# Block 0 of an attention and SwiGLU kernel: k and v loaded in 4 positions by 128 partitions, one root for both halves

## The chip, the cores and the metric

The kernel runs on one core of a Trainium2 chip. The metric is the device time in microseconds (us); the kernel before took 1040.91 us, the median of three runs (1040.91 to 1042.02). One profiled execution of it lasted 1040.28 us, with a span of 1038.5 us in the trace.

The engines are called by their short names: PE (TensorE, matrix products; PEld is its weight load), DVE (VectorE), ACT (ScalarE), POOL (GpSimd), SP (SyncE, which here only issues DMAs).

## What is computed

The reference has two parts. Attention without a softmax, for 8 batches, 8 heads, 576 positions and a head dimension of 64, all in float32:

```
kv  = einsum('bhsd,bhse->bhde', k, v)          # 64 x 64 for each batch and head
o   = einsum('bhsd,bhde->bhse', q, kv)
o   = o / sqrt(mean(o*o, -1) + 1e-6) * g_norm
x   = o with the heads side by side             # 4608 tokens x 512
```

and a SwiGLU layer on these 4608 tokens, with 1536 hidden units. Its three weights come in float64:

```
g   = x @ w_gate;  val = x @ w_val
out = (g * sigmoid(g) * val) @ w_out
```

## The kernel before

The 4608 tokens are worked off in nine blocks of 512 (`NB`, `BLK`). A batch has 576 positions, so block n takes its tokens from batches n-1 and n. `Att(n)` holds the attention of one block, `Ffn(n)` its SwiGLU layer. While the layer of block n runs, attention for block n+1 is fitted in between. From block 1 on the products use a scheme with fewer multiplications (`Up`, `Inner`, `Down`), whose combined weights are made in blocks 0 and 1; block 0 uses plain products (`plain_up`), since its weights only arrive then.

**k^T v.** For each batch, `load_kv(g)` loads k and v for four heads (g = 0, 1), as two pairs of heads j. The 576 positions are cut in two parts r, each on 64 of the 128 partitions, 5 and 4 positions to a partition (`KT` = 5; which part has five alternates with e). That makes 16 DMAs for a batch, each onto 64 partitions. `kv(g)` multiplies them: for each pair j, position c and part r, two matmuls (u, the head in the pair) with 64 rows and 64 columns, each on its own quarter of the PE array. The two parts land in two PSUM tiles; ACT copies the first to SBUF (L292) and DVE adds the second (L293, through the helper at L111). One matmul in float32 appears as two instructions in the trace.

**The head of the kernel.** For block 0 the order is written in `first()`: turn q (transposes on PE with an identity, L307), k^T v, then `half(0)`: the product of q and k^T v for two of the four token tiles (L327), squares on ACT (L338), sums on DVE (L339), `root` (eleven small DVE operations, an inverse square root by three Newton steps, L345 to L357) and `scale` (L364 through the helper at L113). Then q's second half is turned, its product made, and `turn_x(0)` transposes the scaled result (L374) into x, which ACT copies with the gain (L375). The second half's root, scaling and turn (`second()`) come after the first up matmuls `plain_up(0, (0,))`, and the next up group's first half stands between the two halves of the first.

**Weights.** Each float64 weight piece (128x512 words) is loaded by `Words` into one of four `ld` buffers, and `round_to` makes float32 of it: two ACT operations (L144 for the lower word, L146 for the upper), then four on DVE (L147, L152, L153, L157). `weights(upto)` does so for the pieces in the order g0, v0, g1, v1, and so on, and keeps four loads ahead.

**Order.** The instructions of an engine are put in order by a list scheduler that follows the order of the program where operands and buffers allow; it knows nothing of the real chip. `tc.issue_after(ins)` puts everything traced in its block that runs on the engine of `ins` behind `ins` on that engine; it orders one engine's instructions and makes no engine wait for another. DMAs from SP and from ACT (`nc.sync`, `nc.scalar`) are two queues.

Of the kernel before, what the change touches and what calls it, by code (L numbers as in the profile page):

```python
# [8 lines left out]
F32 = mybir.dt.float32  # L9
U32 = mybir.dt.uint32  # L10
I32 = mybir.dt.int32
OP = mybir.AluOpType
ACT = mybir.ActivationFunctionType

P = 128
# [3 lines left out]
def kernel(  # L19
# [41 lines left out]
    nc = tc.nc  # L61

    B, H, S, D = q.shape
    NT, DM = out.shape
    FF = moe_w_gate.shape[1]
    T = 4
    BLK = P * T
    HB = BLK // 2
    HD = DM // 2
    NB = NT // BLK  # L70
    NS = DM // P
    NF = FF // P
    NP = NF // 2
    KT = 5
    LD = 2 * (2 * KT - 1) * D
    eps = 1e-6
    assert NT == B * S and NT == NB * BLK and NB == B + 1 and S - BLK == BLK // B
    assert 2 * D == P and H == 2 * NS and (2 * KT - 1) * D == S and NS == 4

    def pool(name, bufs, **kw):  # L80
        return ctx.enter_context(tc.tile_pool(name=name, bufs=bufs, **kw))
# [37 lines left out]
    class Words:  # L119
# [18 lines left out]
        def round_to(self, dst):  # L138
            halves = self.raw.rearrange("p (f w) -> p f w", w=2)
            low, high = halves[:, :, 0], halves[:, :, 1]  # L140
            room = ring()

            unit = room[:, 0]
            nc.scalar.activation(out=unit, in_=low, func=ACT.Copy, scale=2.0**-51, bias=2.0)  # L144
            mag = room[:, 1].bitcast(U32)
            nc.scalar.activation(out=mag.bitcast(F32), in_=high.bitcast(F32), func=ACT.Abs)  # L146
            nc.vector.tensor_scalar(  # L147
                out=mag.bitcast(F32), in0=mag.bitcast(F32), scalar1=self.LOW, scalar2=self.HIGH,
                op0=OP.max, op1=OP.min,
            )  # L150
            sign = room[:, 2].bitcast(U32)
            nc.vector.tensor_scalar(out=sign, in0=high, scalar1=0x80000000, scalar2=None, op0=OP.bitwise_and)  # L152
            nc.vector.scalar_tensor_tensor(  # L153
                out=mag, in0=mag, scalar=3, in1=sign, op0=OP.logical_shift_left, op1=OP.bitwise_xor
            )
            a, b = self.shape[0], BLK // self.shape[0]
            nc.vector.tensor_tensor(  # L157
                out=dst.bitcast(U32),
                in0=mag.rearrange("p (a b) -> p a b", a=a, b=b),
                in1=unit.bitcast(U32).rearrange("p (a b) -> p a b", a=a, b=b),  # L160
                op=OP.add,
            )
# [3 lines left out]
        "v": (wv, moe_w_val.bitcast(U32).rearrange("(s p) f -> p s f", p=P)),  # L166
        "o": (wo, moe_w_out.bitcast(U32).rearrange("(c p) d -> p c d", p=P)),
    }
    words = {}

    def load_w(name, j):
        src = wviews[name][1]
# [5 lines left out]
    def round_w(name, j):  # L178
        if name == "o":
            dst = wo[:, j : j + 1, :]  # L180
        else:
            dst = wviews[name][0][j // 2][:, :, P * (j % 2) : P * (j % 2 + 1)]
        words.pop((name, j)).round_to(dst)

    class Att:

# [18 lines left out]

        def place_kv(self, g, i):

            n = (2 * g + i) * LD
            if self.n == 0:
                return self.room.rearrange("p f t -> p (f t)")[:, n : n + LD]  # L210
            if self.n == 1 and g == 0:
                return self.room[:, n : n + LD]
            return ld_pool.tile([P, LD], F32, name="ld")

        def load_kv(self, g):


            if self.n == B:
                return
            for i, (views, src) in enumerate(((self.k, k), (self.v, v))):  # L220
                tile_ = self.place_kv(g, i)
                for e in range(2):
                    j, s0 = 2 * g + e, 0
                    for r in range(2):
                        m = KT - (r != e)
                        at = 2 * D * (KT - r) * e
                        t = tile_[r * D : (r + 1) * D, at : at + 2 * D * m].rearrange("p (h x) -> p h x", h=2)
                        queue = nc.scalar if self.n == 0 and i else nc.sync
                        queue.dma_start(
                            out=t,  # L230
                            in_=src[self.n, 2 * j : 2 * j + 2, s0 : s0 + m * D].rearrange("h (p t) d -> p h (t d)", t=m),
                        )
                        views[j, r] = t.rearrange("p h (t d) -> p h t d", t=m)
                        s0 += m * D

        def load_quarters(self, i):

# [35 lines left out]
        def kv(self, g):  # L273


            if self.n == B:
                return
            if g == 0:
                self.kv_ps = [m_psum.tile([P, NS, D], F32, name="m") for _ in range(2)]
            for e in range(2):  # L280
                j = 2 * g + e
                for c in range(KT):
                    for r in range(2):
                        m = KT - (r != e)
                        for u in range(2 if c < m else 0):
                            nc.tensor.matmul(  # L286
                                self.kv_ps[r][u * D : (u + 1) * D, j, :], lhsT=self.k[j, r][:, u, c, :],
                                rhs=self.v[j, r][:, u, c, :], start=(c == 0), stop=(c == m - 1),
                            )
            if g == 1:  # L290
                dst = kvs[self.n % 3]
                nc.scalar.copy(out=dst, in_=self.kv_ps[0])  # L292
                self.kv_made = add(nc.vector, dst, self.kv_ps[1], dst)  # L293

        def turn_q(self, i, pools=None):

# [16 lines left out]
        def product(self, i, pools=None):  # L313

            pools = pools or (m_psum, m_psum)
            self.ps[i] = [pool.tile([P, 2, NS, D], F32, name=pool.name[0]) for pool in pools]  # L320
            for t in range(2):
                for j in range(NS):
                    for b, _, p0, p1 in self.parts(2 * i + t):
                        for p in range(p0, p1, D):
                            for u in range(2):
                                rows = slice(u * D, (u + 1) * D)
                                nc.tensor.matmul(  # L327
                                    self.ps[i][u][p : p + D, t, j, :],
                                    lhsT=self.qt[rows, 2 * i + t, j, p : p + D], rhs=kvs[b % 3][rows, j, :],
                                    start=True, stop=True,  # L330
                                )
            if self.z is None or 0 < self.n < TURNED:
                self.z = st_pool.tile([P, 2, 2, 2, NS], F32, name="z")
            if i == 0:
                self.sq = ring().rearrange("p f (t j d) -> p f t j d", t=2, j=NS)
            for u in range(2):
                sq = self.sq[:, 2 * i + u]
                self.squared = nc.scalar.activation(out=sq, in_=self.ps[i][u], func=ACT.Square)  # L338
                nc.vector.tensor_reduce(out=self.z[:, i, u], in_=sq, axis=mybir.AxisListType.X, op=OP.add)  # L339

        def root(self, i, k=1):

# [84 lines left out]

        def first(self):
            self.turn_q(0, (b_psum, c_psum))
            for g in range(2):  # L430
                self.kv(g)
            self.half(0)
            squared = self.squared
            self.turn_q(1, (b_psum, c_psum))
            with tc.issue_after(self.scaled.ins):
                self.product(1, (b_psum, a_psum))
            self.turn_x(0)
            return squared, self.scaled

        def second(self):  # L440
            self.root(1)
            self.scale(1)
            self.turn_x(1)
            return self.scaled

        def turn(self):
            for i in range(2):
# [536 lines left out]
    def weights(upto):  # L984
        nonlocal rounded
        while rounded < min(upto, len(pieces)):
            load_weights(rounded + 4)
            round_w(*pieces[rounded])
            rounded += 1
# [6 lines left out]
    blocks = [Att(n) for n in range(NB)]  # L996
    blocks[0].room = h_pool.tile([P, NF, BLK], F32, name="h")
    blocks[0].load_q(0)
    for g in range(2):
        blocks[0].load_kv(g)  # L1000
    blocks[0].load_q(1)
    load_weights(4)
    squared, scaled = blocks[0].first()
# [1 line left out]
    for n in range(NB):  # L1005
        ffn = Ffn(n, blocks[n])
        nxt = blocks[n + 1] if n + 1 < NB else None
        if n == 0:
# [1 line left out]
            with tc.issue_after(squared.ins), tc.issue_after(scaled.ins):  # L1010
                weights(2)
            ffn.plain_up(0, (0,))
            scaled = blocks[0].second()
            for f in range(NF):
                with tc.issue_after(scaled.ins), tc.issue_after(blocks[0].copied.ins) if f else ExitStack():
                    weights(2 * (f + 2))
                if f == 1:
                    ffn.plain_up(1, (0,))
                    ffn.plain_up(0, (1,))
                ffn.plain_up(f, (1,)) if f == 1 else ffn.plain_up(f) if f else None  # L1020
            weights(len(pieces))
            pairs = wo.rearrange("p (j e) d -> p e j d", e=2)
            t2(pairs[:, 0, :, HD:DM], pairs[:, 1, :, HD:DM], pairs[:, 0, :, 0:HD])
# [22 lines left out]
            ffn.up({4: third, 8: two_thirds} if nxt else {})  # L1046
        if nxt:
            nxt.turn()
        if n + 2 < NB:
            blocks[n + 2].load_kv(0)  # L1050
        if TURNED - 2 <= n < NB - 2:
            ffn.loads = blocks[n + 2].load_q
# [2 lines left out]
                    ffn.loads(i)  # L1055
        ffn.down(nxt)
        if n == 0:

            with tc.issue_after(nxt.halves[0].ins):
                for j in range(NP):  # L1060
                    t2(wv[j][:, 0:2], wv[j][:, 2:4], wg[j][:, 0:2])
# [31 lines left out]
```

## Time and profile before

| part of the span | us | from |
|---|---|---|
| PE busy | 1011.3 of 1038.5 | busy table |
| DVE busy | 701.3 | busy table |
| ACT busy | 231.8 | busy table |
| first k^T v matmul | 8.47 | order of time |
| first product of q and k^T v | 17.75 | order of time |
| first transposes of x | 25.32 | order of time |
| first up matmul | 29.13 | order of time |
| k^T v of block 1 | 115.81 | order of time |
| k^T v of block 2, first half | 181.86 | order of time |
| PE waits for an ACT result in block 1 | 2.55 before 201.53 | order of time |

How to read it: an engine's busy time says how much it does, not whether anything waits for it. PE is busy for 97% of the span, so time is lost where PE stands still, or where it runs at a lower granted clock. The rows in order of time show the first: each names its start, and in brackets the idle time before it with what ended that. In the head (the first 38 us) many short steps follow one another on PE, ACT and DVE; there the date at which a step starts says more than its length. DMA rows tell when a transfer was issued; when it landed is seen from the instruction that waited for it.

### The profile page before, as it was taken

The page shows a single profiled execution, that of the slowest core. Times are in us where ns is not written, and L with a number is a line of the kernel's source. Part 1 is how long each engine was busy: PE and PEld are TensorE (multiplying, and loading weights), DVE is VectorE, ACT ScalarE, POOL GpSimd, SP SyncE. Part 2 cuts the span into 40 slices and gives each one's busy share as a digit, 9 for nine tenths or more (in the row PEclk, how much of TensorE's full clock was granted, in tenths as well). Part 3 has the DMA queues.
Part 4 walks back from the last instruction along what each step waited for, and adds up shares of the span by engine and source line. Part 5 has one row for each costly group of instructions (what it writes and reads, how often), then busy time and mean ns, then how long its engine had stood idle before and what let it go on. Part 6 is the DMA issues. An engine that isn't in the chain of part 4 may idle for free.

```text
span 1038.5 us, 21544 instructions
## 1 busy us (share of the span) xinstructions
PE 1011.3 (97%) x8588; PEld 907.9 (87%) x8588; DVE 701.3 (68%) x1202; ACT 231.8 (22%) x357; POOL 368.5 (35%) x280
## 2 busy tenths in 40 slices
PE   4899999999999999999999999999999999999998
PEld 3644688788899989998999899988999899989997
DVE  2999696789656866675766666684668566856661
ACT  3666111122212111121111111211122111212110
POOL 0000443435024631563147305640455136512670
PEclk9899999999999999999999999999999999999999
DMA  9689604765468556864676377726862666166611
GB/s 213 184 260 266 164 1 127 186 191 147 129 179 242 135 111 191 243 162 80 197 239 192 59 204 226 222 47 173 250 194 51 164 206 187 29 152 211 191 31 41
DMA packets 255044, 168.16 MB, mean 162 GB/s; under 512 B 124640, under 2 KB 230240, under 8 KB 254944
## 3 DMA queue, kind: packets, MB, share of 16 engines
q1 hardware_dynamic: 228384, 162.45, 56.5%
q10 hardware_dynamic: 26496, 4.33, 2.4%
q8 instruction: 68, 1.11, 0.5%
q14 instruction: 32, 0.26, 0.1%
q0 software_dynamic: 64, 0.00, 0.0%
HBM read 138.02 MB, written 22.41 MB: 154 GB/s over the span
## 4 chain that ended last, share of the span: by engine, by line
PE 91%; DVE 4%; DMA 2%; issue 1%; POOL 1%; ACT 0%; SPq 0%; DVEq 0%; POOLq 0%; ACTq 0%
PE b L662 25%; PE b L513 20%; PE c L662 12%; PE c L513 10%; PE a L662 6%; PE a L513 5%; PE b L956 4%; PE c L956 4%; PE m L286 2%; PE m L327 1%; DMA w<-t 1%; DVE xi L112 1%; DVE r L111 1%; DVE r L112 1%; DMA h<-in_k_dram 1%
## 5 line engine op out<-in xcount | busy, mean ns | idle before, releaser
L111 POOL TENSOR_TENSOR r<-r 128x256 f32<-128x256 f32 (+1 forms) x105 | 110.8, 1061 | 308.5 <-DVE r L111 233.3
L111 DVE TENSOR_TENSOR r<-b,r 128x512 f32<-128x512 f32 (+1 forms) x273 | 161.8, 605 | 64.2 <-PE b L662 59.1
L112 POOL TENSOR_TENSOR t<-wo 128x512 f32<-128x512 f32 x81 | 115.2, 1446 | 195.5 <-DMA t<-in_q_dram 107.8
L111 DVE TENSOR_TENSOR r<-c,r 128x512 f32<-128x512 f32 (+1 forms) x179 | 108.3, 617 | 89.1 <-PE c L662 49.5
L662 PE MATMUL b<-x,t 128*128 128x128 f32 x1092 | 151.0, 275 | 0.0
L662 PEld LDWEIGHTS b<-x,t 128*128 128x128 f32 x1092 | 136.5, 192 | 0.6 <-DVE r L111 0.2
L111 DVE TENSOR_TENSOR r<-a,r 128x512 f32<-128x512 f32 (+1 forms) x99 | 62.4, 630 | 109.2 <-PE a L513 65.8
L662 PE MATMUL c<-xi,t 128*128 128x128 f32 x840 | 112.2, 275 | 0.3 <-DVE xi L111 0.3
L113 POOL TENSOR_TENSOR h<-r 128x1024 f32<-128x1024 f32 (+1 forms) x40 | 81.4, 2050 | 87.6 <-DVE r L111 74.5
L662 PEld LDWEIGHTS c<-xi,t 128*128 128x128 f32 x840 | 102.8, 192 | 0.4 <-DVE xi L111 0.4
L513 PE MATMUL b<-wo,h 128*128 128x256 f32 x432 | 99.4, 382 | 0.1
L513 PE MATMUL b<-t,h 128*128 128x256 f32 x432 | 96.9, 381 | 0.0
L513 PEld LDWEIGHTS b<-t,h 128*128 128x128 f32 x432 | 81.4, 190 | 11.3 <-issue 0.2
L513 PEld LDWEIGHTS b<-wo,h 128*128 128x128 f32 x432 | 80.0, 190 | 12.6 <-DVE h L113 2.5
L676 ACT COPY r<-b 128x512 f32<-128x512 f32 x63 | 36.9, 585 | 212.8 <-PE b L662 212.8
L662 PE MATMUL b<-xi,t 128*128 128x128 f32 x588 | 79.7, 276 | 0.0
L662 PEld LDWEIGHTS b<-xi,t 128*128 128x128 f32 x588 | 72.4, 192 | 0.0
L662 PE MATMUL b<-x,wg 128*128 128x128 f32 x336 | 52.7, 279 | 0.2 <-DVE x L112 0.2
L662 PE MATMUL b<-x,wv 128*128 128x128 f32 x336 | 51.4, 275 | 0.0
L956 PE MATMUL b<-x,wg 128*128 128x512 f32 (+1 forms) x112 | 45.5, 550 | 3.0 <-ACT r L146 1.9
L513 PE MATMUL c<-t,s 128*128 128x256 f32 x216 | 48.3, 380 | 0.0
L513 PE MATMUL a<-wo,h 128*128 128x256 f32 x216 | 48.3, 379 | 0.0
(133 smaller groups left out, 1583.6 us busy)
## 6 DMA issues: line engine op xcount, KB each, us to landing
t<-w SPq DMA_DIRECT2D x336, 256.0 KB, 3.5
out_dram<-r SPq DMA_DIRECT2D x17, 512.0 KB, 3.1
ld<-in_moe_w_gate_dram SPq DMA_DIRECT2D x12, 512.0 KB, 4.8
ld<-in_moe_w_val_dram SPq DMA_DIRECT2D x12, 512.0 KB, 4.8
ld<-in_moe_w_out_dram SPq DMA_DIRECT2D x12, 512.0 KB, 5.3
w<-t SPq DMA_DIRECT2D x18, 256.0 KB, 2.4
w<-xi SPq DMA_DIRECT2D x12, 384.0 KB, 3.1
ld<-in_k_dram SPq DMA_DIRECT2D x26, 160.0 KB, 3.5
```

The source lines that it names most:

```text
L111: add = lambda e, o, a, b: e.tensor_tensor(out=o, in0=a, in1=b, op=OP.add)
L112: sub = lambda e, o, a, b: e.tensor_tensor(out=o, in0=a, in1=b, op=OP.subtract)
L113: mul = lambda e, o, a, b: e.tensor_tensor(out=o, in0=a, in1=b, op=OP.mult)
L286: nc.tensor.matmul(self.kv_ps[r][u * D : (u + 1) * D, j, :], lhsT=self.k[j, r][:, u, c, :], rhs=self.v[j, r][:, u, c, :], start=(c == 0), ...
L327: nc.tensor.matmul(self.ps[i][u][p : p + D, t, j, :], lhsT=self.qt[rows, 2 * i + t, j, p : p + D], rhs=kvs[b % 3][rows, j, :], start=True, ...
L513: nc.tensor.matmul(banks[e][:, e], lhsT=lhsT, rhs=rhs, start=first and i == 0 and (e == 0 or banks[0] is not banks[1]), stop=i == self.ste ...
L662: nc.tensor.matmul(ps[:, i, f], lhsT=self.weight(o, p, f), rhs=self.operand(o, p), start=first and (i, f) == (0, 0), stop=True, skip_group ...
L676: nc.scalar.copy(out=dst, in_=ps)
L956: nc.tensor.matmul(t, lhsT=w[f // 2][:, i, P * (f % 2) : P * (f % 2 + 1)], rhs=x[:, i, of], start=(i == 0), stop=(i == NS - 1),)
```

## The change

**k and v of block 0** are loaded by a function of their own, `load_first_kv`. Positions 0 to 511 go to all 128 partitions, four positions to each, in four DMAs on SP's queue (k and v, four heads each). The last 64 positions go to 64 partitions in four DMAs on ACT's queue. `first_kv` multiplies head by head: four matmuls with 128 rows and 64 columns, and one with 64 rows for the last positions, 40 in all, where there were 72. The result needs no addition: ACT copies four heads, DVE the other four.

**Later batches** are loaded with nine positions to a partition (`KT` = 9), a pair of heads on each 64 partitions: 8 DMAs a batch, where there were 16. `kv(g)` runs over the nine positions with four quarters of the array each time; two ACT copies bring out the result, and the addition on DVE goes.

**One root for both halves.** `first()` makes both products before one `root(0, 2)`, then scales both halves. Between the two products the first weight piece is rounded: on DVE it stands behind the first half's sums and ahead of the second half's. The lower word of a piece is now converted after the upper (L144 and L146 trade places). q's second half is turned behind the first product.

**The first up groups** are plain: both halves of f = 0, then f = 1, without the exchange of before.

**Block 2's first k and v loads** come after `down` of block 0 in the program, where they stood ahead of it.

The purpose is to have the first k^T v sooner, to take DVE work out of the head, and to use all quarters of PE in the later k^T v.

```
+        def load_first_kv(self):
+            room = self.room.rearrange("p f (h x) -> p (f h) x", h=2)
+            most = {"k": room[:, 0:H], "v": room[:, H : 2 * H]}
+            ...
+            for g in range(2):
+                heads, rows = slice(NS * g, NS * (g + 1)), slice(D * g, D * (g + 1))
+                for x, src in (("k", k), ("v", v)):
+                    nc.sync.dma_start(
+                        out=most[x][:, heads], in_=src[0, heads, 0:BLK].rearrange("h (p t) d -> p h (t d)", t=T)
+                    )
+                    nc.scalar.dma_start(out=last[x][rows], in_=src[0, heads, BLK:S].rearrange("h p d -> p h d"))
+        def first_kv(self):
+            banks = [m_psum.tile([P, 2, D], F32, name="m") for _ in range(2)]
+            for h in range(H):
+                j, u = divmod(h, 2)
+                ps = banks[j // 2]
+                for c in range(T + 1):
+                    ...
+                    nc.tensor.matmul(
+                        ps[u * D : (u + 1) * D, j % 2], lhsT=k, rhs=v, start=(c == 0), stop=(c == T)
+                    )
+            nc.scalar.copy(out=kvs[0][:, 0:2], in_=banks[0])
+            nc.vector.tensor_copy(out=kvs[0][:, 2:4], in_=banks[1])
...
         def kv(self, g):
-            for e in range(2):
-                j = 2 * g + e
-                for c in range(KT):
-                    for r in range(2):
-                        m = KT - (r != e)
-                        for u in range(2 if c < m else 0):
-                            nc.tensor.matmul(
...
+            for c in range(KT):
+                for r in range(2):
+                    k, v = self.k[2 * g + r], self.v[2 * g + r]
+                    for u in range(2):
+                        nc.tensor.matmul(
...
-                nc.scalar.copy(out=dst, in_=self.kv_ps[0])
-                self.kv_made = add(nc.vector, dst, self.kv_ps[1], dst)
+                for r in range(2):
+                    nc.scalar.copy(out=dst[:, r], in_=self.kv_ps[r])
...
         def first(self):
             self.turn_q(0, (b_psum, c_psum))
-            for g in range(2):
-                self.kv(g)
-            self.half(0)
-            squared = self.squared
-            self.turn_q(1, (b_psum, c_psum))
-            with tc.issue_after(self.scaled.ins):
+            self.first_kv()
+            self.product(0)
+            with tc.issue_after(self.multiplied.ins):
+                self.turn_q(1, (b_psum, c_psum))
+            with tc.issue_after(self.squared.ins), tc.issue_after(self.summed.ins):
+                weights(1)
+            with tc.issue_after(words_made[-1].ins):
                 self.product(1, (b_psum, a_psum))
+            self.root(0, 2)
+            for i in range(2):
+                self.scale(i)
             self.turn_x(0)
...
             ffn.plain_up(0, (0,))
-            scaled = blocks[0].second()
+            blocks[0].turn_x(1)
             for f in range(NF):
-                with tc.issue_after(scaled.ins), tc.issue_after(blocks[0].copied.ins) if f else ExitStack():
+                with tc.issue_after(blocks[0].copied.ins):
                     weights(2 * (f + 2))
-                if f == 1:
-                    ffn.plain_up(1, (0,))
-                    ffn.plain_up(0, (1,))
-                ffn.plain_up(f, (1,)) if f == 1 else ffn.plain_up(f) if f else None
+                ffn.plain_up(f) if f else ffn.plain_up(0, (1,))
...
-        if n + 2 < NB:
+        if 0 < n < NB - 2:
             blocks[n + 2].load_kv(0)
...
         ffn.down(nxt)
         if n == 0:
+            blocks[2].load_kv(0)
```

## The prediction

> **What bounds the kernel now.** I read the page first: its busy shares and its 40 slices.
>
> ```profile
> PE   4899999999999999999999999999999999999998
> PEclk9899999999999999999999999999999999999999
> ```
>
> TensorE (PE) is full from the second slice on, so outside the first 26 us a change pays only by what it takes off PE. Then I read the busy time by stretches, to see where the hole at the start lies and what DMA moved meanwhile.
>
> ```profile
> 12.00:14.00 2.00, 2.00 (x14) 1.61 (x12) 0.69 (x1) 0.00 (x0) 0.00 (x0) 1.00 1.11 235
> 18.00:20.00 2.00, 0.96 (x64) 0.82 (x55) 0.41 (x1) 1.04 (x2) 0.00 (x0) 1.00 1.08 347
> 22.00:25.00 3.00, 0.17 (x12) 0.04 (x4) 2.60 (x11) 2.78 (x6) 0.00 (x0) 1.00 0.59 184
> 25.00:29.00 4.00, 1.95 (x8) 1.55 (x8) 4.00 (x10) 2.88 (x5) 0.00 (x0) 0.55 0.15 30
> ```
>
> The columns are stretch, length, busy PE, weight loads, DVE, ACT, POOL, granted clock, DMA share, GB/s. k and v arrive at 235 GB/s, while the weights (18 to 20 us) arrive at 347. From 22 to 29 us PE does 2.1 us of work, DVE works nearly throughout, and the clock falls. Third, TensorE alone in order of time (start, length, line, result, tile size, shape, count; in brackets the idle time before and what ended it).
>
> ```profile
> 11.02 1.11 PE L286 MATMUL m<-h 64*64 64x64 f32 x20 [1.68 <-DMA h<-in_k_dram]
> 12.06 1.11 PE L307 MATMUL b<-ident,ld 128*128 128x128 f32 x4
> 13.96 2.93 PE L286 MATMUL m<-h 64*64 64x64 f32 x114
> 25.32 1.95 PE L374 MATMUL m<-ident,r 128*128 128x128 f32 x8 [3.14 <-DVE r L113]
> 29.13 3.48 PE L956 MATMUL b<-x,wg 128*128 128x256 f32 x8 [1.87 <-ACT r L146]
> 115.81 1.28 PE L286 MATMUL m<-xi 64*64 64x64 f32 x69
> ```
>
> k^T v waits for DMA and ends near 16.9; after it come the product (17.75), the root and the scaling, and x^T is turned only at 25.32. Last, the chain of waits, which names the second hole:
>
> ```profile
> 34.43 0.42 DVE h L113
> 34.85 0.34 DVE r L147
> 35.19 0.34 DVE r L152
> 35.52 0.33 DVE r L147
> 35.86 0.60 DVE r L153
> 36.46 0.34 DVE r L152
> 36.80 0.61 DVE wg L157
> 37.45 1.99 PE b L956 x8
> ```
>
> PE waits for a weight piece whose rounding DVE put behind the second root. After 37.45 it runs on, 24 up groups of 8 matmuls of 512 columns at 3.43 us in sum (82.4 us), until k^T v of block 1 at 115.81. So the head is a chain of latencies, and I cost it by one date: the start of that k^T v. Without waits, at full clock, the up work would have had to start at 115.81 - 82.4 = 33.4.
>
> **What the Trainium skill says.** "SBUF — State Buffer", Door 1: a transfer's bandwidth goes by how many SBUF ports its partitions reach, and partitions 64 to 127 lie on other ports than 0 to 63, so 64 partitions reach half of them. The trace agrees in direction: the k and v loads, 64 partitions each, ran at 235 GB/s against 347 for weights on 128. "TensorE: Matmul & The Clock Gate", LDWEIGHTS: loading time goes by columns, not by contraction; so 128 rows by 64 columns should cost what 64 by 64 does. No run here shows that shape. The same page, The HAM clock gate: an idle window of about 3.4 us halves the clock, a busy one restores it, and windows run free of the kernel. The trace agrees: 0.50 between 26 and 32 us, after the hole at 22. "TensorEngine Tiling (Array Packing)", Key Properties: changing the tiling mode drains TensorE. The trace: in block 1, eight matmuls from 180.04 at 216 ns end issuing at 181.77, k^T v starts at 181.86 and the next full-array matmul at 183.17, 1.31 later against 1.14 in the run of k^T v below: 0.09 in, 0.17 out.
>
> **The change, part by part.**
>
> *Loads of block 0.* 2.10 MB of k and v now go to 128 partitions: at 347 GB/s 6.0 us. The last 64 positions (0.26 MB) and the first q (0.52 MB) go in 256-byte rows; the stretches from 4 to 6 us moved 172 to 206 GB/s, I take 190: 4.1 us. From the first byte at 2.0, with 0.7 for landing: heads 0 to 3 at 9.8, all at 12.8, where before the last k came at 16.09. A gain of 3.3 us in data, if PE can use it.
>
> *k^T v of block 0.* One step of a 64-column tile: block 1's first half takes 1.14 us (115.81 to 116.95) for 20 steps of up to four tiles side by side, 57 ns each. At the half clock I take 114: the four transposes from 12.06 took twice what they take later. Forty matmuls are 80 instructions (each is two in the trace), but five for one head lie on the same column half and follow each other: 80 steps, not 40. And each head goes from 128 rows to 64 and back. A change costs between 0 and 0.15 us (the mean of 0.09 and 0.17 is 0.13); I take 0.06, as only the rows change, and keep both ends. Before 15.1 PE is cold, and a head takes 10 x 0.114 + 0.12 = 1.26: from 9.8, 4.2 heads. The other 3.8 take 0.57 + 0.12 = 0.69 each: end at 17.7. The two copies run side by side, about 0.3 (128x256 took 0.37 and 0.42), with hand-overs 0.4: product from 18.1, against 17.6 before, where copy and add took 0.83. The ends are 17.4 and 19.3.
>
> *One root, and the piece between.* From the ready k^T v: product 1.3, squares 0.6 each, the second sum ends at +3.2. ACT then has two copies and the piece's Abs (0.55 each); DVE rounds it in 1.9 (0.34 + 0.34 + 0.60 + 0.61), to +5.9. What is queued behind that on DVE are the sums of the second half, waited for by the root: 1.2, to +7.1. The root, 11 small operations of 0.21 as from 21.60 to 23.97, to +9.5 (twice the elements took 192 ns against 175). Two scalings 1.3, to +10.8. The turn at half clock 1.97 and the second copy 0.7: x is there at +13.5, or 31.6. The second scaling ends at +12.1, so its eight transposes (1.7 cold) lie beside the copies. Removed are one root (2.3) and the hole before 37.45: piece g0 is done, v0 follows the scaling in 2.1, long before its matmuls, and g1 has all of half 0 and half 1 of the first up group (7 us) to be done in. If ACT takes the piece ahead of the copies, +0.65.
>
> *Result for the head.* 31.6 + 82.4, plus the half clock: before, 29.13 to 32.1 cost 1.5; as PE is nearly unbroken from 28.9 on, I take 0.9. k^T v of block 1 starts at 114.9: a gain of 0.9.
>
> *Blocks 1 to 7.* A position group of five and four left 20 steps a half; nine positions are 18. On PE, which is full: 2 x 57 ns x 14 halves = 1.6 us. Their loads are 8 instead of 16 a block, and DVE loses an add of 0.42 for a second short copy on ACT: nothing, as PE runs beside them without a gap. Block 2's first loads, issued from 110 on, are needed at 181.86: their move costs nothing, hidden by 60 us of other work.
>
> Sum: 1040.9 - 0.9 - 1.6 = 1038.4.
>
> **The rivals.**
>
> *The head gives all back (chance 0.28).* The high price of the shape changes (k^T v at 19.3), ACT taking the piece first (+0.65), and a clock window that costs 1.7: 19.3 + 14.15 + 82.4 + 1.7 = 117.5, 1.7 later than now, which the 1.6 of the later blocks repays: 1041.0. For it: 80 steps in a row where four tiles ran side by side. Against: most of them lie before 15.1, when data were missing anyway.
>
> *A new wait in the first up group (0.20).* Half 1 of f = 0 now follows half 0 in the same PSUM bank; before, f = 1 came between. If its matmuls wait for Silu and the DVE multiply, and that stands behind a rounding of 2.0: +2.0 on the case above, and if the tiles already overlap at the seams, only 0.5 comes from the later blocks: 1040.9 + 1.7 + 2.0 - 0.5 = 1044.1, slower. Against: Silu has the wv matmuls to run in, the multiply the next wg ones.
>
> *Block 1's hole closes too (0.10).* PE stands 2.55 us before 201.53, behind a DVE and DMA chain, and then runs 3.4 us at clock 0.50 (1.7 lost). If the shifted start lets that chain through: 1038.4 - 4.2 = 1034.2. Against: nothing in that chain is touched.
>
> **How the numbers follow.** The forecast has 0.42, the likeliest, and gives the time. Range 1034.4 to 1043.6: it takes in the rival that gives back, both prices of the shape change (-0.7, +1.2) and the clock window's phase (about 1.5 either way), and leaves half of each outer case. Faster: 0.42 + 0.10 = 0.52; same 0.28; slower 0.20.
>
> **What would show it.** The last k of block 0 near 13 us and GB/s near 350 before it; k^T v as 80 instructions with no DMA wait in its second half, ending near 17.7; one set of 11 root operations, ending near 27.6; the first 128x256 up matmul near 31.6 and no wait for a rounding after it; k^T v of block 1 near 114.9; and in later blocks 1.03 us for each half. A k^T v ending past 19, or a wait of PE on ACT or DVE after the first up group, would make it wrong.

## The result, and the profile after

The changed kernel took 1050.99 us (median; 1049.97 to 1053.46) against 1040.97 for the one before: ratio 1.0097, with a 95% interval of 1.0079 to 1.0116. It is 10 us slower, where 1038.4 had been forecast. The page shows where to look. In the first slice (26 us) PE is fuller than before, in the second emptier, and the second has lost clock as well; a dent in the ninth lies at waits that before had too.

```profile
PE   6699999989999999999999999999999999999998
...
PEclk9799999999999999999999999999999999999999
```

PE alone in order of time, with the columns of the same view above:

```profile
10.43 11.51 PE L241 MATMUL m<-h 128*64 128x64 f32 x79 [3.44 <-DMA h<-in_v_dram]
...
22.43 1.97 PE L350 MATMUL m<-kv,r 64*64 64x64 f32 x56 [0.16 <-DVE kv L245]
...
34.21 1.97 PE L397 MATMUL m<-ident,r 128*128 128x128 f32 x8 [6.96 <-DVE r L113]
36.10 2.90 PE L978 MATMUL b<-x,wg 128*128 128x256 f32 x8
...
40.56 1.04 PE L397 MATMUL m<-ident,r 128*128 128x128 f32 x8
...
45.41 4.63 PE L978 MATMUL b<-x,wg 128*128 128x256 f32 x8 [2.34 <-DVE wg L157]
...
126.78 1.28 PE L309 MATMUL m<-xi 64*64 64x64 f32 x72
```

Three things are to be seen. k^T v runs for 11.5 us without a wait, and ends at 22.0, where 17.7 had been forecast. After the products PE stands 6.96 us until the root and the scaling are through (3.14 before, for the first half alone). And after the first half of the first up group there is a second hole, of 2.34 us, for the rounding of a weight piece. k^T v of block 1, the date by which the prediction counted, starts at 126.78 instead of 115.81: 11.0 later. The rest of the span gives 1.3 back, since the spans differ by 9.7 (1048.2 against 1038.5).

The busy time by stretches (columns as above) shows the data side of the first stage:

```profile
10.00:14.00 4.00, 3.57 (x27) 3.13 (x28) 0.00 (x0) 0.00 (x0) 0.00 (x0) 1.00 1.20 298
14.00:18.00 4.00, 4.00 (x29) 3.30 (x29) 0.00 (x0) 0.27 (x1) 0.00 (x0) 1.00 1.13 319
...
27.00:34.00 7.00, 0.25 (x19) 0.11 (x8) 6.23 (x18) 2.71 (x6) 0.00 (x0) 0.80 0.45 145
...
45.00:52.00 7.00, 6.59 (x14) 4.63 (x15) 4.80 (x10) 5.13 (x10) 0.00 (x0) 0.53 0.93 289
```

From 10 to 14 us DMA moves 298 GB/s, where the prediction had read 235 before; taken from 8 to 12, while the last of k and v are under way, it is 323 and 346, against 237 and 231 before. The last of k and v landed at 13.4 instead of 16.1, so the loads do what they were meant to do. (The 319 behind that are q's second half and weights.) But PE, "busy" for the whole of 14 to 18 us, gets only 29 instructions done in it: 138 ns each, where the single 64-column step was priced at 57 (full clock) or 114 (half). From 45 to 52 us the granted clock is 0.53: the second hole was followed by a stretch at half clock, where before had full clock. (The profile has no clock record ahead of the first change of the clock, at 24.3 us here, and prints 1.00; that the clock was half until then is read from lengths. The product from 22.43 takes 1.97 us, and 1.15 in a run where the clock was up.)

What set the second hole is told by the chain of waits of this stretch (start, length, what):

```profile
39.00 1.73 PE c L978 x8
40.72 0.45 PE m L397 x4
41.20 0.48 ACT x L398
...
42.35 0.68 ACT r L145
43.05 0.43 DVE r L147
...
43.82 0.60 DVE r L153
...
44.75 0.61 DVE wg L157
45.37 0.04 issue
45.41 0.79 PE b L978
```

The second half of x is turned only behind the first 16 up matmuls; ACT copies it; only then does ACT get to its share of piece g1 (L145), then DVE rounds it, then PE goes on.

### The profile page after: what moved, and what is told of

Same layout as the page of the kernel before. It is cut to its first block, busy times and chain, and to the rows that moved or that the text cites. A ratio compares the mean times of both kernels' runs of the same rounds, so it can differ in the third digit from the quotient of the medians.

```text
span 1048.2 us, 21289 instructions
## 1 busy us (share of the span) xinstructions
PE 1019.2 (97%) x8508; PEld 910.0 (87%) x8508; DVE 700.2 (67%) x1183; ACT 231.9 (22%) x363; POOL 369.1 (35%) x280
## 4 chain that ended last, share of the span: by engine, by line
PE 92%; DVE 5%; DMA 1%; issue 1%; ACT 0%; SPq 0%; POOL 0%; DVEq 0%; POOLq 0%; ACTq 0%
PE b L684 25%; PE b L535 20%; PE c L684 12%; PE c L535 10%; PE a L684 6%; PE a L535 5%; PE b L978 4%; PE c L978 4%; PE m L309 2%; PE m L350 1%; PE m L241 1%; DVE xi L112 1%; DVE r L112 1%; DMA h<-in_v_dram 1%; PE m L397 1%
```

## The experiments

Two questions: why k^T v takes 11.5 us, and why so much is lost behind it. A change of shape is one from 128 rows to 64 or back, counted here as two for each group of 64-row matmuls; the last group is followed by the product, which has 64 rows too, so 15 of the 16 lie within k^T v. Times are medians; before ran beside each, at 1040.3 to 1041.0. "Interval" is that of the ratio to before.

### The first k^T v: the order of heads

**Pairs of heads side by side.** The two heads of a pair go to the two column halves in turn; 8 changes of shape instead of 16.

```
-            for h in range(H):
-                for c in range(T + 1):
+            for h, c in [(2 * j + u, c) for j in range(NS) for c in range(T + 1) for u in range(2)]:
```

> The changed kernel with block 0's k^T v walked by pairs of heads, so that two matmuls on the two column halves of PE follow each other; the loads and all else stay. Theory A (k^T v runs one 64-column tile at a time, which both doubles its steps and keeps PE at half clock although it is busy all the time): 40 steps instead of 80 and 8 changes of shape instead of 16, so k^T v takes some 5 to 6 us instead of 11.5, the clock is 1.0 before 20 us, and the time falls by 6 to 8 us from 1051, to 1043 to 1045. Rival B (the joint root and the wait for piece g1 make the loss; k^T v is hidden in data that come late): k^T v still waits for data, gain under 2 us, 1049 or more. Rival C (the clock stays low because of the free-running window, not because of half an array): k^T v at about 6 us, but the clock still 0.5 at 20 us.

Measured: 1044.72 (interval 1.0022 to 1.0063), 6.3 less than the change.

**Heads one at a time, few changes.** The 128-row matmuls of four heads first, then their four 64-row ones; 4 changes of shape.

```
+            order = [(NS * g + i, c) for g in range(2) for i in range(NS) for c in range(T)]
+            ends = [[(NS * g + i, T) for i in range(NS)] for g in range(2)]
+            for h, c in order[0:16] + ends[0] + order[16:32] + ends[1]:
```

> The changed kernel with the same one-after-another heads, but the four matmuls with 128 rows of four heads first and then their four with 64 rows, so 4 changes of shape instead of 16. If each change costs about 0.19 us at half clock, as the changed kernel's trace shows, k^T v takes 11.5 - 12 x 0.19 = 9.2 us and the time falls by 2 to 2.5 us, to 1048.5. Theory A: the clock stays 0.5 to the end of k^T v, as half the array is still used at a time. Rival C: the clock may rise earlier. Rival B: no change.

Measured: 1043.38 (1.002 to 1.0034). In order of time on PE, first the run with pairs, then that with few changes:

```profile
11.31 2.99 PE L240 MATMUL m<-h 128*64 128x64 f32 x40 [4.35 <-DMA h<-in_v_dram]
14.58 2.88 PE L240 MATMUL m<-h 128*64 128x64 f32 x38 [0.28 <-DMA h<-in_v_dram]
...
17.97 1.97 PE L349 MATMUL m<-kv,r 64*64 64x64 f32 x56 [0.17 <-DVE kv L244]
```

```profile
11.13 5.73 PE L242 MATMUL m<-h 128*64 128x64 f32 x74 [4.51 <-DMA h<-in_v_dram]
...
17.43 1.15 PE L351 MATMUL m<-kv,r 64*64 64x64 f32 x56 [0.37 <-DVE kv L246]
```

Both take little more than half of 11.5 us. The second never sets out to put two heads side by side, and is as quick as the first: that a head fills only half of the columns is not what made the change slow. In its single records steps come 60 and 47 ns apart in turn, at half clock, where one head's alone are 107 apart. I read that as one head and the next, on the other half, interleaved: PE lays neighbours side by side by itself where no change of shape lies between. The product behind it takes 1.15 us, at full clock (from 16.2 us); in the run with pairs 1.97, and the clock rises only at 21.0.

**Both edits together.**

```
+            most = lambda g: [(NS * g + 2 * j + u, c) for j in range(2) for c in range(T) for u in range(2)]
+            for h, c in most(0) + ends(0) + most(1) + ends(1):
```

> The changed kernel with both edits in block 0's k^T v: pairs of heads side by side, and 4 changes of shape instead of 16. Theory A2 (the changes of shape keep PE's clock at half: where they take a quarter of the time, as in the changed kernel and with 8 changes side by side, it stayed low; with 4 it rose): clock 1.0 by 17 us, k^T v ends with the data, near 16, 1 us ahead of the run with fewer changes alone: 1042 to 1042.6. If side by side adds nothing once the changes are gone: 1043.4.

Measured: 1044.73 (1.0026 to 1.0044), no better than the one edit. k^T v ends no sooner (17.4, against 17.0), since its second half now waits 0.57 us for v, until 14.85.

**No last positions.** The eight 64-row matmuls are left out (the sums over the last 64 positions are missing); the order of heads is the change's.

```
-                for c in range(T + 1):
+                for c in range(T):
```

> The kernel after, with the eight 64-row matmuls of the last 64 positions of block 0 left out (the sums over these positions are missing): heads one at a time as in the change, but no change of shape between them. Theory A (the changes of shape cost: the drains themselves, the overlap of one head with the next on the other column half, and the clock): k^T v takes under 6 us, ends near 17, the clock is full by 18 us, and the time is like e2's, 1043 to 1045. Theory B (a head alone fills only half of the columns, and that keeps steps and clock slow): 64 steps of 107 ns and the wait for the second half's data, end at 17.8 to 18.5, half clock until 21 us or later, 1046 to 1048.

Measured: 1044.0 (1.0017 to 1.0041). From its order of time:

```profile
12.06 2.55 PE L241 MATMUL m<-h 128*64 128x64 f32 x32 [5.13 <-DMA h<-in_v_dram]
15.20 2.29 PE L241 MATMUL m<-h 128*64 128x64 f32 x32 [0.58 <-DMA h<-in_v_dram]
```

The 64 steps take 4.84 us, where in the change they and 16 more take 11.51. The 16 steps themselves are worth 16 x 0.107 = 1.7; the other 5.0 us are what the changes of shape cost. 2.8 of it are the pauses at the changes, which I call drains: in the change's single records a head's first 64-row step starts 0.244 us after the one before it and its second 0.162 later, and back 0.242 and 0.159, where steps are else 0.107 apart: 0.38 a head above four such steps, so 0.19 for each of 15 changes. Nearly all of the rest is the overlap of a head with the next: 64 steps of 0.107 would be 6.85, not 4.84. Both kernels run k^T v at half clock nearly throughout, so the clock has no part in this.

**The clock.** In the five runs that keep the sixteen changes (the change itself and four of the kernels here) the first record of a full clock lies at 23.9 to 28.5 us, behind the whole k^T v, though PE stood nowhere in it; that is 13.9 to 17.9 us after its start. In the six with the new loads and four changes or none it comes 5.0 to 9.6 us after the start (in four of them, too, behind the end of their shorter k^T v; these four run the same k^T v and scatter from 6.8 to 9.6), in the one with eight 9.7. The Trainium skill says ("TensorE: Matmul & The Clock Gate", The HAM clock gate) that a busy window restores the clock; here 11.5 us that the profile calls busy did not. That the drains count as idle fits all of these runs, but it is an argument: no run varies the drains alone.

**Before's first k^T v in the change.** Loads and k^T v of block 0 as before, all else as in the change.

```
-        def load_first_kv(self): ...    # 4 positions on 128 partitions
+        def load_first_kv(self): ...    # 5 and 4 positions on 64, as load_kv before
```

> The changed kernel, but block 0's k and v loaded and multiplied as before (5 and 4 positions on 64 partitions each, four quarters of PE, copy and add); joint root, piece between, plain first up groups and nine positions later stay. Theory A: k^T v ends near 17 with PE at full clock, so the product starts 4.5 us earlier and runs at full clock: 1044.5 to 1046, and what is left above 1041 is the joint root and the wait for g1. Rival B: the loss stays, 1048 or more.

Measured: 1044.07 (1.0019 to 1.0042). Undoing the part is worth 6.9 us, as much as mending it (6.3 to 7.6), so the sooner data bring nothing that shows. And 3.1 us of loss against before stay, though the later batches gain (see below), so there is a second cause.

### What follows k^T v: root, piece and turn

**Two roots.** The change's loads, k^T v and later batches, with before's order of block 0 (two roots, no piece between, exchanged up groups), with the change's order of heads and with both edits of it:

```
-            self.product(0) ... weights(1) ... self.product(1) ... self.root(0, 2)
+            self.half(0) ... self.product(1) ... self.turn_x(0)     # second(): root(1), scale(1), turn_x(1)
```

> The changed kernel's loads, first k^T v and later batches, with the order of the kernel before in block 0: a root for each half, no piece rounded between, the first two up groups exchanged. If the joint order costs 3 us on its own, as the run with the old first k^T v says (1044.1 against 1040.9), this is 3 to 4 us below the changed kernel, 1047. If the two parts only add up through the clock: nearer 1045. If the order is neutral with late data: 1050.

> As the run with two roots, and block 0's k^T v side by side with 4 changes of shape. Data are there at 14.4 against 16.1 in the kernel before, so the product may start at 16.5 to 17 instead of 17.75, and the later batches give 0.7: 1039 to 1039.8, ahead of both kernels. If the data's gain is lost to the slow clock and the changes: 1040.5 or more.

Measured: 1048.82 (1.0054 to 1.0089) and 1040.91 (0.9997 to 1.0014): 2.2 and 3.8 less than their counterparts with the change's order. The second cause lies here. In the latter the first half of x is turned at 25.10, 8.2 us after the first matmul of the product; in the change 12.6 (21.58 to 34.21). The two runs undo the joint root, the piece and the plain up groups together; what follows takes them apart.

**g1 later.** The rounding of g1 and v1 is placed behind the second half of f = 0 in the program, alone and with both edits of the heads.

```
+                if f == 0:
+                    ffn.plain_up(0, (1,))
                 with tc.issue_after(blocks[0].copied.ins):
                     weights(2 * (f + 2))
-                ffn.plain_up(f) if f else ffn.plain_up(0, (1,))
+                if f:
+                    ffn.plain_up(f)
```

> The changed kernel, with the rounding of g1 and v1 placed after the second half of the first up group in the program instead of ahead of it. In the changed kernel that half's second matmul waits for g1, a piece it does not read, and after that wait PE runs 6 us at half clock. Theory D (the wait is a dependency on the neighbouring columns of the same tile, and the slow clock follows from the hole): the wait of 2.3 us is gone, the clock does not fall again after 45 us, time down by 3 to 5 us to 1046 to 1048. Rival (the wait moves to the first matmul that does read g1): under 1 us.

> The kernel after with heads side by side, four changes of shape, and the rounding of g1 and v1 placed after the second half of f = 0 (e5 and e6 together). In e6 the last of these took the hole before the up matmuls away, but block 1's q came no sooner. Theory A (the loads of block 1 set the pace there whatever the head does): k^T v of block 1 starts 1 to 2 us sooner than in e5 (118.2), then PE waits 1 to 3 us for q; 1043.5 to 1045, no better than e5's 1044.7. Theory B (the wait for q came from e6's late head alone): no wait there, 1041 to 1042.5.

Measured: 1050.25 (1.0073 to 1.0106) and 1043.94 (1.002 to 1.0039), only 0.7 and 0.8 less than without. From the order of time of the first, at the second half of f = 0 and at block 1's q:

```profile
43.01 1.99 PE L978 MATMUL b<-x,wg 128*128 128x256 f32 x8 [0.34 <-ACT x L398]
...
127.78 0.60 PE L330 MATMUL c<-ident,t 128*128 128x128 f32 x4 [2.16 <-issue]
```

The hole is gone: the 256-column matmuls run from 43.01, though g1's last rounding step begins only at 45.74. So in the change they had waited for a piece that they do not read; it lies in the same tile as g0, in the neighbouring columns, and stood ahead of them in the program. k^T v of block 1 started 4.5 us sooner (122.25). But then PE waited ahead of the second pair of block 1's q turns, 2.16 us here and 3.26 in the other run, with 3.4 us at half clock after each:

```profile
122.88 1.01 PE L331 MATMUL c<-ident,t 128*128 128x128 f32 x4 [3.26 <-DVE r L335]
```

The gain turned into a new wait. It was not for q: the last quarter of q, issued at 116.6 (110.6 in the other run), had landed at 122.7 (116.7), 5.0 and 6.1 us before PE went on. The profile's releasers explain nothing either ("issue" means that it shows none; the DVE copy of the other run was done 0.5 us earlier). What fits is in the DMA packets: a fetch of instructions, one packet of 16 KB on the queue q8, lands at 126.4 (121.2), and PE goes on 1.4 us later (1.7). In all seven runs that wait more than 0.2 us at this place, for 0.24 to 3.26, PE goes on 1.3 to 1.7 us after such a packet; in the change it is 0.49 us. So PE probably stood for its own next instructions, but no run varies the fetch: this is argued, not shown.

**No piece between the products.** The one line that rounds g0 between them goes, and with it the order of the second product. With both edits of the heads, and then in the change itself:

```
-            with tc.issue_after(self.squared.ins), tc.issue_after(self.summed.ins):
-                weights(1)
-            with tc.issue_after(words_made[-1].ins):
-                self.product(1, (b_psum, a_psum))
+            self.product(1, (b_psum, a_psum))
```

> The kernel after with heads side by side and four changes of shape (as in e5, 1044.7 us), and no weight piece rounded between the two products: g0 is rounded after the two halves are scaled. It splits the joint root from the piece. In e5 the first half's sums end at 21.2, DVE then rounds the piece until 23.87 and the root begins at 25.18; but the second half's squares end only at 23.6. Theory A (the joint root itself costs, the piece only fills time in which DVE would wait for the second half): the root begins at most 1.3 us sooner, x is turned near 27.8, and the first up matmul, which now waits for g0's rounding (about 2.3 us after the scaling), starts at 31 or later, no sooner than e5's 30.96: 1043.5 to 1046. Theory B (the piece's 2.75 us on DVE are what the root loses): x turned at 26.4, first up before 29.8, 1042 or less.

> The change itself (k^T v head by head with its sixteen changes of shape), with one thing taken out: no weight piece is rounded between the two products, and the second product has no order on its engines. In e10 the same edit took 5.3 us off e5 (1039.4 against 1044.7): both halves of x were turned in the time in which PE waited for g0's rounding, g1's came 4.4 us sooner, and the hole before the first 512-column matmuls was gone. Theory A (the place of the piece is worth the same here, whatever k^T v does): x^T of both halves in one run, no hole of 2.3 us after it, k^T v of block 1 near 122 instead of 126.8, 1045 to 1047. Theory B (with k^T v ending at 21.9 the later work falls into a new wait, as in e6, and little is left): k^T v of block 1 near 122, then over 2 us of wait for q, 1048.5 to 1050.5.

Measured: 1039.43 (0.9978 to 0.9994), faster than before; and 1044.62 (1.0029 to 1.0057), 6.4 less than the change. For the first, the forecast of theory A was right in its dates (x turned at 27.86, first up 31.60) and wrong in the time; theory B was right in the time and wrong in the dates. What neither saw is in the order of time of the second:

```profile
22.05 1.98 PE L350 MATMUL m<-kv,r 64*64 64x64 f32 x56 [0.16 <-DVE kv L245]
...
32.76 3.86 PE L397 MATMUL m<-ident,r 128*128 128x128 f32 x16 [5.88 <-DVE r L113]
36.50 2.50 PE L975 MATMUL b<-x,wg 128*128 128x256 f32 x8
38.84 1.89 PE L975 MATMUL c<-x,wv 128*128 128x256 f32 x8
40.82 1.99 PE L975 MATMUL b<-x,wg 128*128 128x256 f32 x8
...
120.00 1.28 PE L309 MATMUL m<-xi 64*64 64x64 f32 x72
```

With the edit, the first up matmul is 0.4 us later than in the change, and k^T v of block 1 is 6.8 sooner. g0, now rounded behind the scaling, is ready late, and in the time in which PE would wait for it both halves of x are turned, 16 transposes in one run; the hole at 43 us is gone, and no half clock follows.

**The second turn first.** The piece stays between the products, but the second half of x is turned ahead of the first up matmuls.

```
-            ffn.plain_up(0, (0,))
-            blocks[0].turn_x(1)
+            blocks[0].turn_x(1)
+            ffn.plain_up(0, (0,))
```

> The change with the piece still rounded between the products, but with the second half of x turned ahead of the first up matmuls, as it came out by itself in e10 and e14. It asks which effect of the piece costs the 6.4 us that e14 gained. Theory A (the piece's place sent PE's second turn and ACT's copies of it behind the first up matmuls, and so the lower word and the rounding of g1): x turned at 34.2 as now, first up near 38, no hole of 2.3 us before the 512-column matmuls, k^T v of block 1 near 122, 1045 to 1046.5. Theory B (what counts is the 2.75 us on DVE ahead of the second half's sums and the root): first up near 38, 1.9 later than now, and g1 still waited for: 1049 to 1051.

Measured: 1045.72 (1.0032 to 1.0057), 5.3 of the 6.4 us. From its order of time:

```profile
34.80 3.86 PE L397 MATMUL m<-ident,r 128*128 128x128 f32 x16 [6.41 <-DVE r L113]
38.46 2.02 PE L978 MATMUL b<-x,wg 128*128 128x256 f32 x8
...
42.85 1.99 PE L978 MATMUL b<-x,wg 128*128 128x256 f32 x8 [0.65 <-ACT h L983]
```

x is turned no sooner than in the change and the first up matmul is 2.4 us later, and still the kernel is 5.3 us faster. g1's last rounding step begins at 41.59, instead of 44.67. So most of the loss was not DVE's time for the piece, but the place of the second turn: behind the up matmuls, it put ACT's copies, and so g1, late.

### The later batches, and the parts put together

**Nine positions alone.** Before, with only the later batches of the change.

```
+                    t = tile_[r * D : (r + 1) * D].rearrange("p (h x) -> p h x", h=2)
+                    ...    # batches 1 to 7: 9 positions to a partition, kv(g) over c, r, u, two copies
```

> The kernel before, with nine positions a partition for batches 1 to 7 only (loads of 8 DMAs, all four quarters of PE each time, two ACT copies); block 0 and its order stay as before. The prediction's step: 1.6 us off PE, 1039.3. From the changed kernel's trace, where k^T v of block 1 takes 2.28 us against 2.40: 0.1 us for each of seven blocks, 1040.2. If these parts cost something (the copies on ACT, the DMA of longer rows): 1041 or more.

Measured: 1039.08 (0.9978 to 0.9991): 1.85 us less than before's 1040.93 in the same runs. Only about half of that is PE's own work: summed over batches 1 to 7, the time from the first to the last k^T v matmul of each stretch falls from 17.01 to 16.06 us. A part of the difference between the two profiled runs is the clock. Both have a hole in block 1, of 2.55 and 2.65 us; before has 3.4 us at half clock behind it, this run none. What makes up the rest of the 1.85 in the medians is open.

**The good parts.** Before's loads and k^T v of block 0, one root for both halves without the piece, nine positions later.

> The change with before's loads and k^T v of block 0 (as in e3, 1044.07) and no piece rounded between the products (as in e10 and e14); one root for both halves and nine positions in the later batches stay. Theory A (the parts add up, and the new first loads bring nothing even with few changes of shape): e3 less the 5.3 to 6.4 that this edit took off e5 and the change: 1037.5 to 1039, no later than e10's 1039.4. Theory B (once the piece is out of the way, the sooner product of e10, 16.9 against 17.3, shows in the time): 1040 or more.

Measured: 1038.04 (1037.67 to 1038.75), ratio 0.9972, interval 0.9961 to 0.9983: faster than both kernels. It is no slower than the run with the new loads (1039.43), though that one's product starts 1.1 us sooner. From its order of time:

```profile
18.06 1.16 PE L351 MATMUL m<-kv,r 64*64 64x64 f32 x64 [0.73 <-DVE kv L111]
...
27.95 3.86 PE L398 MATMUL m<-ident,r 128*128 128x128 f32 x16 [5.87 <-DVE r L113]
31.69 2.96 PE L976 MATMUL b<-x,wg 128*128 128x256 f32 x8
```

Against two roots (1040.91), one root without the piece (1039.43, both with the mended new k^T v) gains 1.5 us, and their intervals (0.9997 to 1.0014, 0.9978 to 0.9994) do not meet: the joint root, with the plain up groups that go with it, was no mistake. Against nine positions alone (1039.08) the best kernel is only 1.0 us faster, and the intervals overlap, so more than half of its gain over before (2.95 us) is that of the later batches, and the rest is not clear of noise.

Dates are those of one profiled execution, whose time stands in the last column but one; the last is the median. The third kernel's profiled execution was the fastest of twelve: its second hole (2.33 us before 39.90) had no half clock after it.

| kernel | k^T v of block 0 ends | first up | k^T v of block 1 | profiled, us | median, us |
|---|---|---|---|---|---|
| before | 16.9 | 29.1 | 115.8 | 1040.28 | 1040.97 |
| the change | 22.0 | 36.1 | 126.8 | 1049.97 | 1050.99 |
| heads mended (both edits) | 17.4 | 31.0 | 118.2 | 1041.24 | 1044.73 |
| piece not between | 21.7 | 36.5 | 120.0 | 1045.37 | 1044.62 |
| both mended | 16.6 | 31.6 | 115.3 | 1039.85 | 1039.43 |
| piece not between, and before's k^T v | 17.3 | 31.7 | 115.3 | 1038.04 | 1038.04 |

The two faults nearly add up: 6.3 for the heads, 6.4 for the piece's place, 11.6 for both together.

## Why the prediction was wrong

**The data: right, a little late.** The second half of k and v was forecast at 12.8 us; in the change it had landed at 13.4, and in the runs that wait for it PE goes on at 13.7 to 15.2, against 16.1 before. As the Trainium skill has it ("SBUF — State Buffer", Door 1), the transfers onto 128 partitions ran quicker (323 to 346 GB/s from 8 to 12 us, against 231 to 237).

**k^T v of block 0: the step that failed first, worth 4.3 us** (product at 22.43 instead of 18.1). "I take 0.06" for a change of shape was wrong by a factor of three: 0.19 at half clock. The upper bound of 0.15 was too low as well; its two durations were taken at full clock. The Trainium skill ("TensorEngine Tiling (Array Packing)", Key Properties) names the drain, and here a change of rows alone brought one. The larger term is the clock: the prediction had PE warm from 15.1; it stayed cold until 24.3, so the last 3.8 heads, priced at 0.69 each, took 1.45. Of the 4.3 us, 2.2 are this clock (3.8 x (1.26 - 0.69)), 1.5 the price of the changes (8 x (1.45 - 1.26)) and 0.6 the later start (10.4 instead of 9.8). That the 80 steps follow one another was right, but only because the drains part them.

**From k^T v to the first up matmul: right as a sum.** +13.5 was forecast, 36.10 - 22.43 = 13.7 measured. That is in part luck: the first half's scaling ended at +11.7 instead of +10.8, and the up matmuls followed the turn's start after 1.9 instead of 2.7, so two errors cancelled.

**From there to block 1: the step that failed most, 7.4 us.** The forecast was 82.4 + 0.9 of half clock; it took 126.78 - 36.10 = 90.7. "Its eight transposes (1.7 cold) lie beside the copies" failed: they came behind the first 16 up matmuls, 1.04 us on a full PE. "g1 has all of half 0 and half 1 of the first up group (7 us) to be done in" failed, as ACT's two operations of g1 stood behind its copies of that turn; holes of 0.34 and 2.34 us, and 6.2 us at half clock after them, which cost 3.1. Together 6.8; 0.6 stays unexplained. The three steps sum to the miss at block 1: 4.3 + 0.2 + 7.4 = 11.9, from 114.9 to 126.8. The rival of a new wait in the first up group put it in the right place, but on Silu and the multiply, at 2.0 us, and without the half clock that followed this hole. The rival in which the head gives all back had the cost of the changes in mind, but its late end of the range, a product at 19.3, was still 3.1 us too early. Block 1's hole did not close: it is 2.47 us before 212.85, though with no half clock behind it in this execution.

**The later batches: right in the time, not in the term.** 1.6 us forecast, 1.85 measured with an interval of about 0.9 to 2.3 (0.09 to 0.22% of 1041). But the forecast had all of it as 0.114 us off each of 14 halves on PE, and PE's part measured 0.95 in sum; that the whole still fits has a part of luck.

**Loads of block 1 and 2 at nothing: right.** In the change q of block 1 had landed at 122.9, 6 us before its first turn, and block 2's k^T v waited for nothing. Nor was q what PE stood for where g1 was moved.

## What to carry to other kernels

Put matmuls of one shape together: an odd-shaped rest after each head cost three times its own work on top of it (5.0 against 1.7 us), while with the rests gathered behind four heads the time could not be told from that without any. When work is moved ahead into a gap, ask which later work the scheduler will pull into or push out of the gap that is left; here the piece that filled a gap on DVE took away the gap on PE in which the second turn would have been free. A first date that improves says little: two kernels whose up matmuls began 0.4 and 2.4 us later than the change's were 6.4 and 5.3 us faster, because nothing stopped PE after them.

## What the runs showed of the hardware

- A change between 128 and 64 rows, with 64 columns in both, cost 0.19 us at half clock each way. It also kept a head on one column half from overlapping with the next on the other: without it a step was 72 ns on average at half clock (the first 32 steps of the run without last positions), with it 107.
- A PE that the profile calls busy throughout can stay at half clock: here for 11.5 us, with two changes of shape in every 1.45 us.
- A hole of 2.3 to 2.7 us in a full PE brought half clock in some executions and not in others: 2.34 us in the change was followed by 6.8 us of it, 2.33 with both edits of the heads by none; 2.55 before by 3.4, 2.65 with nine positions alone by none.
- In seven runs PE stood 0.24 to 3.26 us ahead of block 1's second pair of q turns, and went on 1.3 to 1.7 us after a 16 KB packet of instructions had landed.
